# Sliding-window attention with a gated MLP on one core: new durations, a clock model and new priorities for the planner, and four PSUM banks for the first batch's scores

## The chip, the core and the metric

The kernel runs on one core of one Trainium2 chip. The metric is the device time of one execution in microseconds (us), from repeated executions. Five queues of instructions run side by side: TensorE (PE), VectorE (DVE), ScalarE (ACT), GpSimd (POOL) and SyncE (SP), which issues nearly all DMAs. Each runs its own list in order; semaphores hold an instruction back until what it reads is there. PE's results go to PSUM, which has eight banks.

## The reference

Attention over a window with a few sink keys, then an MLP whose hidden layer passes a three-tap convolution gate (`n_sink` 4, `window` 128, batch 4, 8 heads, sequence 768, head 64, `d_model` 512, `d_ff` 1024, all float32):

```python
scores = np.matmul(q, k.transpose(0, 1, 3, 2)) / np.sqrt(D)
keep = (pos[None, :] < n_sink) | ((rel >= 0) & (rel < window))
scores = np.where(keep, scores, -1e9); scores -= scores.max(-1, keepdims=True)
a = np.exp(scores); a /= a.sum(-1, keepdims=True) + 1e-9
x = np.matmul(a, v).transpose(0, 2, 1, 3).reshape(B, S, H * D)
h = np.maximum(x @ w_in, 0)
gate = 1 / (1 + np.exp(-(w0 * h[s - 1] + w1 * h[s] + w2 * h[s + 1])))
out = (h * gate) @ w_out
```

## The kernel before

Heads go in pairs, a *group* g: four groups a batch, sixteen in all. A group has six query tiles of 128 positions, in two halves of three. For a tile t, PE multiplies queries with the keys of two neighbouring tiles and the sinks (`sc`, one for each head of the pair). DVE copies where the window wraps (COPY_PREDICATED) and masks with a minimum (the custom instruction into `pe`), ACT takes the exponential, DVE the sum and its reciprocal, POOL normalises (`pe<-pe,sm`). PE transposes the result (`pts`), ACT copies it to `pT`, POOL cuts it to the window in two selects, and after three tiles PE multiplies with the values (`px`). The sinks' part goes its own way: ACT and DVE split it (`sk`), PE transposes it (`tk`), and it is added to `px`. ACT and DVE split `px` into a high and a low part (`xH`, `xL`). Batch 0 (groups 0 to 3) works in plain float32 and takes the first halves of all four groups first; later batches use pairs of reduced float32 matmuls (`tq`, `kk`, `nq`: keys and queries split and transposed).

The MLP works in *units*, 8 hidden blocks of 128 for each of 12 chunks of 256 positions, 96 in all. A unit's *first* is 12 matmuls into a bank `ph`; its gate passes ACT, ACT, DVE, DVE, ACT, DVE and twice POOL into `g`; its *second* is twice three matmuls from `g` into the two banks `po`, which collect over a chunk's eight units. The input weights come as 64-bit floats: for each of 16 blocks (`wi`, `wo`) and the taps, ACT and DVE turn them into float32 (lines L716 to L718 on DVE) and split them in two (L729: POOL for `wi`, DVE for `wo`). All this runs while batch 0's attention runs, before the first unit can start.

PSUM's eight banks are named places: `h` 2 (ph and the transposes), `po` 2, `sc` 2, `px` 1, `pts` 1. In SBUF there are 4 buffers `g`, 3 `raww` for raw weights, 3 `st`.

The order of everything is made when the kernel is built. `layout` gives each step a priority (`p.at`): a position in steps of score tiles, with fixed offsets: scores at i, transposes at i + 1, `pv` at i + 2, units from i + 3 with seconds TRAIL = 2 unit spans later, weights at 2, 3, 4, and so on. `Plan.run` then goes through all steps as a list scheduler: each step has a busy time and a time until its result is there; the engine that could start earliest takes, among the steps that are ready within `SLACK`, the one of least priority number. `HOP` and `INTO` are times between engines, `SWITCH` a cost on PE, a DMA lands 2300 ns after the fabric moved it. The order that comes out is the program's, on all engines; the chip keeps it.

## Time and profile before

| | |
|---|---|
| median of 3 runs (lowest, highest) | 524.12 us (523.53, 527.19) |
| the profiled execution's own time | 526.89 us |
| its span, first to last instruction | 525.1 us |
| TensorE's mean granted clock | 0.963 |
| busy: PE, DVE, ACT, POOL | 477.2, 341.4, 343.0, 312.4 us |

A page of the profile gives busy times and a strip of 40 slices; the views behind it list waits (which engine stood still, at which line, and who released it), instructions in order of time, and sums by stretch. A matmul's end is modelled, so PE reads as busy through pauses shorter than a matmul's own latency: one matmul of 512 columns is listed with 0.4 us, and twelve of them in a row take 2.9 us.

### The profile page before, as it was taken

Reading aid. Unit: us, or ns where it says so; the run is one execution under the profiler, and the core shown is the slowest. Engines: PE = TensorE matmul, PEld = TensorE weight load, DVE = VectorE, ACT = ScalarE, POOL = GpSimd, SP = SyncE. Lnnn points to the kernel's source line nnn. Section 1 sums busy time; section 2 is a strip of 40 time slices with the busy share of each in tenths; the row PEclk is TensorE's granted clock in tenths of the full one; section 3 lists DMA queues with packets and bytes.
Section 4 is the critical chain, followed back from the end, with each engine's and each line's share of the span. In section 5 each row is a group of like instructions: output and inputs, shape, how many; then the busy total and the mean of one; then the engine's idle time right before and its main releaser. Section 6 shows DMA issues by size and latency. Waiting matters only on the chain.

```text
span 525.1 us, 10461 instructions
## 1 busy us (share of the span) xinstructions
PE 477.2 (91%) x3149; PEld 398.7 (76%) x3149; DVE 341.4 (65%) x1212; ACT 343.0 (65%) x1086; POOL 312.4 (59%) x614
## 2 busy tenths in 40 slices
PE   2867877999999999989999999989999999999994
PEld 2534665878778878877889788878888888898882
DVE  4668898556676676757577766667665764555552
ACT  3867776676777877776687676767766754545541
POOL 3572786565757686675666657565766655344441
PEclk9977679799999999999999999999999999999999
DMA  5848543435332423413233141324030100101001
GB/s 126 237 134 223 172 144 82 114 86 117 88 78 46 117 60 79 106 40 100 47 85 79 31 118 46 81 66 100 1 88 16 41 2 0 42 0 41 23 20 47
DMA packets 87306, 41.01 MB, mean 78 GB/s; under 512 B 80160, under 2 KB 80184, under 8 KB 87240
## 3 DMA queue, kind: packets, MB, share of 16 engines
q1 hardware_dynamic: 87096, 39.99, 29.1%
q8 instruction: 27, 0.44, 0.4%
q14 instruction: 39, 0.32, 0.2%
q10 hardware_dynamic: 144, 0.26, 0.2%
HBM read 27.60 MB, written 6.29 MB: 65 GB/s over the span
## 4 chain that ended last, share of the span: by engine, by line
PE 67%; DVE 12%; POOL 9%; ACT 6%; issue 3%; DMA 2%; SPq 1%; POOLq 0%; ACTq 0%; DVEq 0%
PE ph L776 22%; PE po L807 19%; PE px L1044 8%; PE sc L950 4%; POOL pe L973 4%; PE pts L990 3%; PE sc L953 2%; PE sc L954 2%; PE px L1052 2%; PE tq L914 2%; DVE e L792 1%; DVE a L793 1%; DVE sc L962 1%; DVE kk L891 1%; DVE pe L963 1%
## 5 line engine op out<-in xcount | busy, mean ns | idle before, releaser
L807 PE MATMUL po<-woH,g 128*128 128x512 f32 x384 | 142.3, 407 | 5.5 <-ACT out L612 2.7
L973 POOL TENSOR_SCALAR pe<-pe,sm 128x132 f32<-128x132 f32 (+1 forms) x192 | 88.6, 471 | 64.2 <-DVE sm L971 52.3
L776 PE MATMUL ph<-xH,wiH 128*128 128x258 f32 (+1 forms) x384 | 111.7, 294 | 2.2 <-ACT sT L612 0.9
L776 PE MATMUL ph<-xL,wiH 128*128 128x258 f32 (+1 forms) x384 | 112.9, 296 | 0.0
L776 PE MATMUL ph<-xH,wiL 128*128 128x258 f32 (+1 forms) x384 | 111.6, 293 | 0.0
L796 POOL TENSOR_SCALAR g<-a 128x256 fp32r<-128x256 f32 x96 | 40.4, 421 | 82.3 <-DVE a L795 60.2
L807 PEld LDWEIGHTS po<-woH,g 128*128 128x128 f32 x384 | 71.3, 188 | 23.7 <-POOL g L797 6.2
L967 ACT ACTIVATE pe<-pe,sm 128x132 f32<-128x132 f32 (+1 forms) x192 | 77.1, 403 | 14.1 <-DVE sm L963 13.2
L776 PEld LDWEIGHTS ph<-xH,wiH 128*128 128x128 f32 x384 | 73.7, 192 | 6.6 <-ACT sT L612 1.8
L776 PEld LDWEIGHTS ph<-xL,wiH 128*128 128x128 f32 x384 | 73.8, 192 | 6.4 <-issue 3.4
L776 PEld LDWEIGHTS ph<-xH,wiL 128*128 128x128 f32 x384 | 73.8, 192 | 3.4 <-issue 0.7
L797 POOL TENSOR_TENSOR g<-a,g 128x256 fp32r<-128x256 f32 x96 | 73.3, 763 | 4.8
L807 PE MATMUL po<-woL,g 128*128 128x512 f32 x192 | 75.7, 395 | 0.0
L962 DVE COPY_PREDICATED sc<-before,sc 128x128 f32<-128x128 int32 x160 | 45.8, 291 | 42.3 <-PE sc L954 29.6
L792 DVE SCALAR_TENSOR_TENSOR e<-hb,cw,a 128x256 f32<-128x256 f32 x96 | 50.6, 527 | 34.4 <-ACT a L614 34.0
L610 ACT ACTIVATE hb<-ph 128x258 f32<-128x258 f32 (+1 forms) x96 | 37.0, 385 | 50.3 <-PE ph L776 49.1
L610 ACT ACTIVATE e<-a 128x256 f32<-128x256 f32 x96 | 40.0, 417 | 35.3 <-DVE a L793 34.8
L795 DVE SCALAR_TENSOR_TENSOR a<-e,hb 128x256 f32<-128x256 f32 x96 | 47.4, 493 | 23.4 <-ACT e L610 22.6
L963 DVE CUSTOM_DVE_ANT_0 pe<-sc,m 128x132 f32<-128x132 f32 (+1 forms) x192 | 53.4, 288 | 5.9 <-PE sc L954 2.4
L996 POOL TENSOR_SCALAR_AFFINE_SELECT pT<-pT 128x256 f32<-128x256 f32 x80 | 36.5, 456 | 34.1 <-ACT pT L612 33.0
L793 DVE SCALAR_TENSOR_TENSOR a<-hb,cw,e 128x256 f32<-128x256 f32 x96 | 51.2, 534 | 4.7 <-DVE e L792 0.5
L614 ACT ACTIVATE a<-hb,cw 128x256 f32<-128x256 f32 x96 | 49.0, 511 | 3.2
(168 smaller groups left out, 934.0 us busy)
## 6 DMA issues: line engine op xcount, KB each, us to landing
raw<-in_q_dram SPq DMA_DIRECT2D x64, 96.0 KB
raw<-in_k_dram SPq DMA_DIRECT2D x64, 96.0 KB
out_dram<-out SPq DMA_DIRECT2D x23, 256.0 KB
kk<-kk SPq DMA_DIRECT2D x24, 198.0 KB
vraw<-in_v_dram SPq DMA_DIRECT2D x24, 192.0 KB
roomL<-in_moe_w_in_dram SPq DMA_DIRECT2D x8, 512.0 KB
roomL<-in_moe_w_out_dram SPq DMA_DIRECT2D x8, 512.0 KB
vraw<-in_v_dram SPq DMA_DIRECT2D x8, 128.0 KB
```

The costliest lines, as they stand in the source:

```text
L610: nc.scalar.activation(o, i, func, **({} if scale is None else {"scale": scale}))
L614: nc.scalar.mul(o, i, scale() if callable(scale) else scale)
L776: nc.tensor.matmul(h.ap[:, 0:W], self.wi[i][:, cc, ff * P:(ff + 1) * P], x[k][:, cc, t0:t1], start=(q == 0), stop=(q == len(prods) - 1))
L792: self.dve(324, lambda: stt(out=e.ap, in0=this(), scalar=cw(1), in1=a.ap, op0=ALU.mult, op1=ALU.add), (hb, a), (e,))
L793: self.dve(324, lambda: stt(out=a.ap, in0=nxt(), scalar=cw(2), in1=e.ap, op0=ALU.mult, op1=ALU.add), (hb, e), (a,))
L795: self.dve(266, lambda: stt(out=a.ap, in0=e.ap, scalar=1.0, in1=this(), op0=ALU.add, op1=ALU.mult), (e, hb), (a,))
L797: self.pool(710, lambda: nc.gpsimd.tensor_tensor(out=g.ap[:, 1], in0=a.ap, in1=f(g.ap[:, 0]), op=ALU.subtract), (a, (g, 0)), ((g, 1),))
L807: nc.tensor.matmul(po.ap[:, 0:c.DM], g.ap[:, k, tt * P:(tt + 1) * P], w[:, ff, :], start=(ff == 0 and i == 0), stop=(ff == NFF - 1 and i = ...
L962: self.dve(P, lambda pc=pc: nc.vector.copy_predicated(pc.ap[:, KW:SW], self.before.bitcast(I32), pc.ap[:, 0:P]), ("before", pc), (pc,))
L963: self.dve(n + 14, lambda pc=pc, j=j: nc.vector.tensor_tensor_reduce(out=pe()[:, j, cols], in0=pc.ap[:, P:SW][:, cols], in1=mk, op0=ALU.ad ...
L967: p.op("ACT", 395, 505, lambda j=j: nc.scalar.activation(pe()[:, j, cols], pe()[:, j, cols], AF.Exp, bias=sm[:, j:j + 1], scale=-1.0, accu ...
L973: self.pool(350, lambda j=j: nc.gpsimd.tensor_scalar(pe()[:, j, cols], pe()[:, j, cols], sm[:, 8 + j:9 + j], 1.0, ALU.mult, ALU.mult), ((s ...
```

## The change

It has four parts; no instruction of the kernel is added or taken away beyond semaphores, and no arithmetic changes.

**Durations.** The planner's costs are set anew: times between engines, a scale on each engine's busy times (`SCALE`), an extra `CARE` of 37 ns on each crossing, longer q/k loads, transposes with a shorter busy time, `pv` at twice the cost, DMAs that land 1150 ns after the fabric in place of 2300 + 100, and some single steps.

**The clock.** `Plan.run` keeps a count of PE's busy time in stretches and doubles a matmul's cost where its count says that the clock is halved.

**Priorities.** The offsets in `layout` become a table `LAY` of 22 numbers: among them loads of weights earlier ahead of their conversion (`early` 1.5 to 3.95) and conversions spread wider (4.69 + 1.29 n in place of 2 + n), seconds 5.97 spans behind in place of 2, sinks' loads later (i - 1 to i + 3.44), transposes at i + 1.4.

**Banks.** The scores' place gets the two banks of `po` too, until 36 of its tiles have been taken (18 of batch 0's 24 query tiles); then they go to `po`.

```diff
-HOP = {("PE", "PE"): 0, ("ACT", "ACT"): 92, ("DVE", "DVE"): 104, ("POOL", "POOL"): 83, ("SP", "SP"): 0}
+HOP = {("PE", "PE"): 0, ("ACT", "ACT"): 92, ("DVE", "DVE"): 60, ("POOL", "POOL"): 83, ("SP", "SP"): 0, ("DVE", "POOL"): 160}
-SLACK = {"PE": 40, "ACT": 60, "DVE": 60, "POOL": 60, "SP": 0}
+SLACK = {"PE": 0, "ACT": 35, "DVE": 50, "POOL": 99, "SP": 0}
...
+SCALE = {"PE": 1.0, "ACT": 1.03, "DVE": 1.08, "POOL": 1.12, "SP": 1.0}
+CARE = 37.0
+LENT = 36
...
+    def take(self):
+        self.until -= 1
+        self.line.pop(0)
+        got = self.free.pop(0)
+        if self.until == 0:
+            for x in [x for x in self.free if x[1] in self.lent]:
+                self.free.remove(x)
+                self.owner.free.append(x)
+            self.owner.free.sort(key=lambda y: y[0])
+        return got
...
+            busy, late = o.busy * SCALE[e], o.late * SCALE[e]
+            if e == "PE":
...
+                if slow:
+                    busy, late = 2.0 * busy, late + busy
+                used += busy
...
-                o.end = fabric + 2300.0
+                o.end = fabric + 1150.0
...
+        self.place["po"] = Place("po", 0)
+        self.place["sc"] = Place("sc", 2, ("po_0", "po_1"), self.place["po"], LENT)
...
-        p.at = at + TRAIL * span
+        p.at = at + LAY["trail"] * span
...
+LAY = {"w0": 4.69, "w": 1.29, "early": 3.95, "load": 6.0, "v": 1.6, "prep": 4.71, "span": 1.82, "load2": 8.43, "v2": 2.58,
...
-            m.sinks(g // NP, i - 1)
+            m.sinks(g // NP, i - LAY["sink"])
```

What it does to the order is seen in three places. The first is DVE in batch 0, from the scores of group 3's first tile on (`sc3_0_0`: group 3, tile 0, head 0; `wo0w` is a weight block in conversion, `xL` the low part of a finished `px`). Before:

```order
L963 ISA pe3_0_463,sm4_122<-sc3_0_0_528,m0_124 128x128
L963 ISA sm4_122 128x1
L963 ISA pe3_0_463,sm4_122<-sc3_0_1_532,m0_124 128x128
L963 ISA sm4_122 128x1
L729 TENSOR_TENSOR woL_109<-wo0w_505,woH_108 128x512
L716 TENSOR_SCALAR wo1w_558<-wo1l_547 128x512
L962 COPY_PREDICATED sc3_1_0_543<-before_127,sc3_1_0_543 128x128
L717 SCALAR_TENSOR_TENSOR wo1w_558<-roomL_116,wo1w_558 128x512
L969 TENSOR_REDUCE sm4_122<-sm4_122 128x2
L963 ISA pe3_0_463,sm0_118<-sc3_1_0_543,m1_125 128x132
L963 ISA sm0_118 128x1
L718 SCALAR_TENSOR_TENSOR wo1w_558<-wo1l_547,wo1w_558 128x512
```

And in the changed kernel, from the same scores on:

```order
L999 ISA pe3_0_457,sm4_122<-sc3_0_0_426,m0_124 128x128
L999 ISA sm4_122 128x1
L999 ISA pe3_0_457,sm4_122<-sc3_0_1_429,m0_124 128x128
L999 ISA sm4_122 128x1
L999 ISA pe3_0_457,sm0_118<-sc3_1_0_436,m1_125 128x132
L999 ISA sm0_118 128x1
L999 ISA pe3_0_457,sm0_118<-sc3_1_1_443,m1_125 128x132
L999 ISA sm0_118 128x1
L1006 TENSOR_REDUCE sm3_121<-sm3_121 128x2
L998 COPY_PREDICATED sc3_2_0_468<-before_127,sc3_2_0_468 128x128
L1008 RECIPROCAL sm3_121<-sm3_121 128x2
L999 ISA pe3_0_457,sm1_119<-sc3_2_0_468,m2_126 128x132
```

From `sc3_0_0`'s mask to that of `sc3_2_1` (the last score of the first halves) DVE has 12 conversion steps of `wo0` to `wo3` before and 2, of a `wi` block, now. Up to group 3's first `xL` it has 40 conversion steps before and 25 now, but 9 masks of the second halves' scores where it had 6; up to group 3's second `xL` both kernels have all the conversions, but for the last one of the changed kernel.

The second place is PE in batch 1, around the transpose of the sinks' part (`tk4_2`, group 4), which needs what POOL normalised (as `pts4_2` does) and then ACT and DVE. Before:

```order
L990 MATMUL pts4_2_1603<-ident_85,pe4_0_1296 128x128 x2
L953 MATMUL sc4_4_1_1606<-kk4_948,X41_1286 128x260
L954 MATMUL sc4_4_1_1606<-kk4_948,X41_1286 128x260
L1017 MATMUL tk4_2_1618<-identr_90,sk4_0_1610 72x128
L914 MATMUL tq510_1622<-identr_90,nq51_1371 128x128 x3
```

And now:

```order
L1027 MATMUL pts4_2_1584<-ident_85,pe4_0_1256 128x128 x2
L843 MATMUL po0_1_967<-woH_108,g7_1490 128x512
L843 MATMUL po0_1_967<-woL_109,g7_1490 128x512
L843 MATMUL po0_1_967<-woH_108,g7_1490 128x512
L950 MATMUL tq500_1602<-identr_90,nq50_1311 128x128 x3
L1027 MATMUL pts4_3_1611<-ident_85,pe4_1_1543 128x128 x2
L1054 MATMUL tk4_2_1619<-identr_90,sk4_0_1588 72x128
L989 MATMUL sc4_5_0_1622<-kk4_781,X41_1273 128x260
```

More work stands between the two. Over the 24 such places of batches 1 to 3, at most two scores' pairs of matmuls stood between them in 18 before, and in 6 now.

The third place is PE at the end of the program (`ph95` is the last unit's first, `po88_0<-...,g94` a second of unit 94). Before:

```order
L776 MATMUL ph95_6909<-xL1_1696,wiH_106 128x258
L776 MATMUL ph95_6909<-xH1_1695,wiH_106 128x258
L776 MATMUL ph95_6909<-xH1_1695,wiL_107 128x258
L776 MATMUL ph95_6909<-xL1_1696,wiH_106 128x258
L807 MATMUL po88_0_6807<-woH_108,g94_6953 128x512
L807 MATMUL po88_0_6807<-woL_109,g94_6953 128x512
L807 MATMUL po88_0_6807<-woH_108,g94_6953 128x512
L807 MATMUL po88_1_6814<-woH_108,g94_6953 128x512
L807 MATMUL po88_1_6814<-woL_109,g94_6953 128x512
L807 MATMUL po88_1_6814<-woH_108,g94_6953 128x512
L807 MATMUL po88_0_6807<-woH_108,g95_6970 128x512
```

And now:

```order
L812 MATMUL ph95_6904<-xL1_1840,wiH_106 128x258
L812 MATMUL ph95_6904<-xH1_1839,wiH_106 128x258
L812 MATMUL ph95_6904<-xH1_1839,wiL_107 128x258
L812 MATMUL ph95_6904<-xL1_1840,wiH_106 128x258
L843 MATMUL po88_0_6847<-woH_108,g91_6853 128x512
L843 MATMUL po88_0_6847<-woL_109,g91_6853 128x512
L843 MATMUL po88_0_6847<-woH_108,g91_6853 128x512
L843 MATMUL po88_1_6864<-woH_108,g91_6853 128x512
L843 MATMUL po88_1_6864<-woL_109,g91_6853 128x512
L843 MATMUL po88_1_6864<-woH_108,g91_6853 128x512
L843 MATMUL po88_0_6847<-woH_108,g92_6886 128x512
L843 MATMUL po88_0_6847<-woL_109,g92_6886 128x512
```

Between the last first and the last second stand now the seconds of units 91 to 94, where there was that of 94 alone. Beside the attention of batches 1 to 3 a unit's second comes about four units' firsts behind its own first, where it came about one behind.

## Rows read from the trace of the kernel before

**Rows 1.** The page: the span, and two lines of the strip of 40 slices (PE's busy tenths, and the clock that was granted).

```profile
span 525.1 us, 10461 instructions
PE   2867877999999999989999999989999999999994
PEclk9977679799999999999999999999999999999999
```

**Rows 2.** Busy time by stretch (stretch and its length; busy us and instructions of each engine; granted clock, DMA share, GB/s): batch 0, the middle, the stretch of units alone, the end.

```profile
0.00:105.00 105.00, 78.10 (x381) 56.31 (x382) 75.42 (x262) 69.48 (x208) 61.73 (x116) 0.82 0.57 154
105.00:394.00 289.00, 275.99 (x1975) 236.48 (x1974) 196.71 (x755) 207.96 (x695) 187.36 (x384) 1.00 0.30 75
394.00:517.00 123.00, 121.16 (x791) 104.99 (x789) 68.63 (x196) 64.97 (x184) 62.19 (x114) 1.00 0.06 19
```

**Rows 3.** The same view, the five stretches in which the clock was granted at half.

```profile
29.26:36.08 6.82, 5.09 (x20) 2.75 (x19) 3.46 (x17) 3.26 (x11) 6.27 (x10) 0.50 0.26 86
...
39.49:46.32 6.83, 5.88 (x27) 3.64 (x24) 5.49 (x17) 5.67 (x17) 2.42 (x6) 0.50 0.84 237
...
53.15:63.39 10.24, 9.13 (x29) 6.18 (x31) 8.60 (x36) 7.21 (x22) 7.34 (x13) 0.50 0.50 166
...
70.22:77.04 6.82, 6.22 (x24) 5.07 (x26) 6.82 (x20) 4.66 (x13) 6.45 (x9) 0.50 0.53 171
...
90.70:97.52 6.82, 6.31 (x26) 5.33 (x27) 3.63 (x15) 4.69 (x17) 3.94 (x7) 0.50 0.27 62
```

**Rows 4.** Waits from 0 to 105 us: who waited at which line for whom; us in total, times, the longest.

```profile
POOL pe L973 <- DVE sm L971: 19.5, 7, 6.6
DVE sc L962 <- PE sc L950: 10.9, 13, 2.5
...
PE sc L950 <- DVE sm L963: 7.4, 5, 1.8
...
PE trq L853 <- POOL headscale L636: 6.9, 1, 6.9
```

**Rows 5.** DVE in order of time (start us, us, instruction): the mask of the score `sc3_0_0`, the first and the last of the 12 conversion steps that follow, the mask of `sc3_2_1`, and the `xL` of group 3's two halves.

```profile
42.34 0.29 DVE L963 CUSTOM_DVE_ANT_0 pe<-sc,m 128x128 f32<-128x128 f32 x1 [0.64 <-PE sc L950]
...
42.98 0.69 DVE L729 TENSOR_TENSOR woL<-wo0w,woH 128x512 fp32r<-128x512 f32 x1
...
52.70 0.68 DVE L718 SCALAR_TENSOR_TENSOR wo3w<-wo3l,wo3w 128x512 int32<-128x512 int32 x1
...
53.76 0.29 DVE L963 CUSTOM_DVE_ANT_0 pe<-sc,m 128x132 f32<-128x132 f32 x1
...
65.95 0.56 DVE L1063 TENSOR_TENSOR xL<-px,xH 128x384 fp32r<-128x384 f32 x1
...
126.65 0.56 DVE L1063 TENSOR_TENSOR xL<-px,xH 128x384 fp32r<-128x384 f32 x1 [0.35 <-ACT xH L612]
```

**Rows 6.** PE in order of time: three score matmuls that wait for DVE (in brackets the idle time ahead and who ended it), and the first unit's first matmul.

```profile
50.32 0.68 PE L950 MATMUL sc<-kp,X 128*128 128x260 f32 x2 [1.73 <-DVE sm L963]
51.73 0.68 PE L950 MATMUL sc<-kp,X 128*128 128x260 f32 x2 [0.74 <-DVE sm L963]
...
54.20 1.21 PE L950 MATMUL sc<-kp,X 128*128 128x260 f32 x2 [1.80 <-DVE sm L963]
...
64.22 0.39 PE L776 MATMUL ph<-xH,wiH 128*128 128x258 f32 x1
```

**Rows 7.** PE's waits from 97.5 us to the end.

```profile
PE tk L1017 <- DVE sk L1016: 3.9, 8, 0.8
PE po L807 <- ACT out L612: 2.7, 2, 1.5
PE po L807 <- POOL g L796: 1.5, 1, 1.5
PE tk L1017 <- DVE sm L969: 0.9, 2, 0.5
PE po L807 <- POOL g L797: 0.8, 3, 0.3
```

**Rows 8.** The end of the program in order of time: the last unit's last first, ACT behind it, its POOL step, and PE's first matmul of its second.

```profile
513.48 0.28 PE L776 MATMUL ph<-xL,wiH 128*128 128x258 f32 x1
...
513.80 0.39 ACT L610 ACTIVATE hb<-ph 128x258 f32<-128x258 f32 x1 [1.03 <-PE ph L776]
...
516.96 0.40 POOL L796 TENSOR_SCALAR g<-a 128x256 fp32r<-128x256 f32 x1 [2.35 <-DVE a L795]
...
517.42 0.50 PE L807 MATMUL po<-woH,g 128*128 128x512 f32 x1 [1.54 <-POOL g L796]
```

**Rows 9.** Two pieces of the chain that ended last (start us, us, what): twelve matmuls of seconds, and a wait for a small DMA that had been issued.

```profile
231.59 1.77 DMA vsr<-sinkh
...
498.90 2.90 PE po L807 x12
```

**Rows 10.** The groups of instructions: POOL's first step into `g` (busy us, mean ns; idle time ahead and who ended it).

```profile
L796 POOL TENSOR_SCALAR g<-a 128x256 fp32r<-128x256 f32 x96 | 40.4, 421 | 82.3 <-DVE a L795 60.2 <-PE po L807 7.4 <-DVE sm L971 7.0
```

More of the change, by code (lines that the diff above doesn't have):

```diff
@@ L426 @@
 class Op:
-    __slots__ = ("eng", "busy", "late", "fn", "at", "deps", "soft", "outs", "need", "ready", "turns", "size", "narrow", "start", "end", "n", "what")
+    pass
 class Plan:
@@ L508, in run @@
                 mode = o.narrow
+            busy, late = o.busy * SCALE[e], o.late * SCALE[e]
+            if e == "PE":
+                while t >= window + WINDOW:
+                    slow = used < (0.97 if slow else 0.55) * WINDOW
+                    window, used = window + WINDOW, 0.0
+                if slow:
+                    busy, late = 2.0 * busy, late + busy
+                used += busy
+            o.before = []
             for x in o.turns:
                 if x.slot is None:
-                    x.slot = x.place.free.pop(0)[1]
-                    x.place.line.pop(0)
-            o.start, free[e] = t, t + o.busy
-            o.end = t + o.late
+                    _, x.slot, was = x.place.take()
+                    if was is not None:
+                        o.before.append(was)
+            o.start, free[e] = t, t + busy
+            o.end = t + late
             if o.size:
                 fabric = max(t + o.busy, fabric) + o.size / 225.0
-                o.end = fabric + 2300.0
+                o.end = fabric + 1150.0
             for x in o.turns:
@@ L521, in run @@
                 if not x.left:
-                    x.place.free.append((x.end + 60.0, x.slot))
-                    x.place.free.sort()
+                    x.place.back(x.end + 60.0, x.slot, x)
             for d in o.outs:
@@ L584, in turn @@
         pool = self.ps if kind in ("h", "po", "sc", "px", "pts") else self.sb
-        return Turn(self.place[kind], lambda i: pool.tile(shape, dtype, tag=f"{kind}_{i}", name=name))
+        return Turn(self.place[kind], lambda i: pool.tile(shape, dtype, tag=i if isinstance(i, str) else f"{kind}_{i}", name=name))
     def planes(self, name):
@@ L707, in weight @@
         dst = lambda: raw.ap[0:rows, 0:n * (2 if wide else 1)]
-        self.dma(rows * n * (8 if wide else 4), lambda: nc.sync.dma_start(dst() if not wide else dst().bitcast(I32), src if not wide else src.bitcast(I32)), ("room",), (raw,))
+        self.dma(rows * n * (8 if wide else 4), lambda: nc.sync.dma_start(dst() if not wide else dst().bitcast(I32), src if not wide else src.bitcast(I32)), ("room",), (raw,), busy=410)
         p.at = at
@@ L743, in weights @@
             for cc in range(self.NCC):
-                self.weight(f"wi{half}_{cc}", vi[:, cc, s], ats[n], parts=self.wi, spot=(slice(None), cc, s), engine="POOL")
+                self.weight(f"wi{half}_{cc}", vi[:, cc, s], ats[n], parts=self.wi, spot=(slice(None), cc, s), engine="POOL", early=LAY["early"])
                 n += 1
@@ L749, in weights @@
             for ff in range(HF * half, HF * half + HF):
-                self.weight(f"wo{ff}", vo[:, ff, :], ats[n], parts=self.wo, spot=(slice(None), ff), engine="DVE")
+                self.weight(f"wo{ff}", vo[:, ff, :], ats[n], parts=self.wo, spot=(slice(None), ff), engine="DVE", early=LAY["early"])
                 n += 1
@@ L990, in go @@
                 nc.tensor.transpose(pt.ap[:, j, :], pe.ap[:, u, j, NS:KW], c.ident)
-        self.pe(2 * 108, go, ((pe, u, 0), (pe, u, 1)), (pt,), what=f"pts{g}_{t}")
+        self.pe(170, go, ((pe, u, 0), (pe, u, 1)), (pt,), late=216, what=f"pts{g}_{t}")
         own = self.keytile(s, g, t, hf)
@@ L1090, in layout @@
     st = [Ctx() for g in range(NG)]
-    m.weights([2 + i for i in range(17)])
+    m.weights([LAY["w0"] + LAY["w"] * i for i in range(17)])
     kks = [m.turn("kk", [P, 2, T, KW], F32, f"kp{i}") for i in range(2)]
@@ L1122, in layout @@
             for k in range(n):
-                m.unit(m.NFF * lo + k, i + 3 + span * k / n, span / n)
+                m.unit(m.NFF * lo + k, i + LAY["unit"] + span * k / n, span / n)
 def general(c):
```

76 lines of the change are left out of this document (44 added, 32 removed).

## The prediction

> **What bounds the kernel now.** I read the page first: its strip shows PE full from about a quarter of the span on, and uneven before, where the granted clock falls too [rows 1]. The sums by stretch say it in numbers [rows 2]: in the first 105 us PE is busy for 78.1, in the middle for 276.0 of 289, in the last stretch, where only units are left, for 121.2 of 123. So PE bounds the kernel, and what can be won lies in four places: 26.9 us of PE's idle time in the first 105 us, the half clock there, 13.0 us in the middle, and the end behind 517 us. The half clock comes in five stretches, all in the first 97.5 us; PE is busy in them for 5.09 + 5.88 + 9.13 + 6.22 + 6.31 = 32.6 us, which at the full clock would be 16.3 [rows 3].
>
> Then the waits of the first stretch [rows 4]. The 6.9 us for `headscale` are the program's beginning and stay. The others are one picture: DVE waits 10.9 us for PE's scores, PE 7.4 us for DVE to free a score's bank, POOL 19.5 us for DVE's sums. No engine is full (DVE, the fullest of the helpers, works 75.4 of 105 us [rows 2]); they wait for each other, because each runs its list in order. The timeline of DVE shows why [rows 5]: between the masks of `sc3_0_0` and `sc3_2_1`, at 42.34 and 53.76 us, stand 12 conversion steps of the output weights. PE stands meanwhile at scores three times, 1.73 + 0.74 + 1.80 = 4.3 us, and the first unit starts at 64.22 us [rows 6]. Those weights are not needed before a unit's gate is through. From 97.5 us on PE's waits are short and of a few kinds: 3.9 + 0.9 us at the transposes `tk`, 2.7 us at `po` for the copies out, 1.5 + 0.8 at `po` for `g` [rows 7]; of these the 1.5 is the wait at the very end [rows 8].
>
> **The change part by part.** Nothing is removed from any engine's work, so every gain is a wait that goes, and the sum is one of waits.
>
> *Batch 0's order.* Ten of the 12 conversion steps leave the gap between those two masks. One takes 0.69 or 0.68 us where the timeline shows it [rows 5], the shift among every four less; I take 0.6. Up to group 3's first `xL`, which the first unit needs whole, DVE has 15 conversions less, 9 us, and three scores' masks more, each a copy and a mask of about 0.3 us, 2 us in all: 7 us less DVE work ahead of the first units. The work comes back later: before group 3's second `xL` (at 126.65 us now [rows 5]) both kernels must have done nearly all conversions. There it lies beside the units' matmuls, in the 30 us that DVE idles in this stretch; without that room the 7 us would be paid again.
>
> *Four banks.* With two banks PE can be one tile ahead of DVE; with four, two tiles. That meets the 7.4 us of PE and the 10.9 us of DVE [rows 4], two sides of one thing, so they don't add. At least the 4.3 us of the three waits should mostly go; at most all 10.9. Part of it is the same time as the conversions above, since PE waited for a bank while DVE converted. I take 5 beside the 7. The loan costs the units' seconds nothing as long as the first of them comes after the 18th tile; in the new order it stands behind four units' firsts, so those cover it.
>
> The Trainium skill speaks against this part: "TensorE: Matmul & The Clock Gate", section "HAM oscillation", tells of a kernel in which more PSUM buffers brought no further gain once its matmuls ran without long pauses. By that the 5 us would be 0 and the time 511; the waits for banks listed above say that here the pauses are still there.
>
> *The start together:* 7 + 5 = 12 us. The lower bound is 4 (only the three waits), or 0 if all is given back; the upper is 7 + 10.9, plus a third of the clock's 16.3 us if PE's denser work keeps two of the five half stretches away [rows 3]: 23. That the planner knows the halving moves no work by itself, so it gets no term.
>
> *The middle.* More work now stands between `pts` and `tk`. The waits at `tk` come where ACT's and DVE's small steps take longer than what stands there; such places fall from 18 to 6 of 24, so I take two thirds of 4.8 us: 3.2. The seconds stand four units behind their firsts in place of one, which takes away the 0.8 us at `po` for `g`. Together 4. Against it: new priorities can make new waits anywhere, and the planner now believes that a DMA lands 1.15 us after the fabric, where the chain has 1.77 us of waiting behind a small one's issue [rows 9]. Sinks are loaded later too, so three batches may each stand 0.6 us or more. Bounds: 3 lost (these and as much again) to 12 won (nearly all of PE's 13.0 us idle [rows 2]).
>
> *The end.* The last first ends 0.12 us after 513.48 (its neighbours' spacing, since 12 seconds take 2.90 us at 512 columns [rows 9] and these have half), the last second starts at 517.42 [rows 8]: 3.8 us for the gate's chain through ACT, DVE and POOL, covered by six seconds, 1.45 us. Now 24 seconds stand there, 5.8 us, and the chain is hidden: 2.4 us won. What is late next is only the copy and store of the last tiles, which stay. Bounds 1.5 (the wait that is listed) and 2.4.
>
> *Sum:* 12 + 4 + 2.4 = 18.4 us. From the profiled execution's own time, 526.89 us, that gives 508.5. This execution was 2.8 us above the median of the three runs, 524.12; from the median it is 505.7, and I say 506.
>
> **The rivals.**
>
> *Given back.* DVE's deferred conversions, 15 of 59, return before group 3's second `xL`. If PE then waits for scores as it did before, only later, the 12 us go and the middle and the end remain: 524.1 - 6.4 = 517.7. For it: all conversions but one are still ahead of that `xL`. Against it: PE has units to run by then, and DVE's idle 30 us are four times the 7.
>
> *More than that.* DVE's whole wait for scores goes and the clock stays up longer: 23 us in the start, with the rest 29: 494.5. For it: all three engines wait for each other [rows 4], so one loosened link moves all. Against it: the chain from a score through POOL to `px` is as long as it was.
>
> *Slower: the buffers of `g`.* There are four. With seconds four units behind, POOL's step into `g` of unit n needs the buffer that the second of unit n - 4 frees, at about the time when the first of unit n is done. POOL runs in order, so its normalising of scores waits behind that step, then `pts`, `pT`, `px`. Before, POOL already waited 7.4 us for this [rows 10]. Some 64 units run beside attention. If 0.29 us of such waiting reached PE at each, the 18.4 us would be lost; at 0.5 us each, 32 us, the time is 524.1 - 18.4 + 32 = 538. Against it: POOL has 100 us of idle time in the 289 us of the middle [rows 2], and the planner holds these buffers in its account.
>
> **How the numbers follow.** The sum as worked out, with its start between 6 and 17 and a middle between 0 and 8: 0.67, 498 to 514, at 506. Given back: 0.14, 514 to 522, about 518. More: 0.11, 488 to 498. Slower: 0.08, 525 to 545. A measurement tells about 1%, 5.2 us, from no change. Faster than 518.9 are the first and the third and about a third of the second: 0.83; the rest of the second and what of the fourth stays under 529.4 is within: 0.10; slower 0.07. The range 495 to 518 leaves out the slower case, part of the second and the best of the third.
>
> **What would show it.** In the new profile the first unit should start at 50 to 57 us in place of 64.22, group 3's second `xL` come 8 to 17 us before 126.65, PE's waits for DVE at scores fall below 3 us, and DVE's for PE's scores by half. The middle should list under 2 us at `tk`, and the end no wait of PE for `g`. If the first unit is early but that `xL` is not, it was given back. If POOL lists far more than 7.4 us of waits for PE at its step into `g` and PE waits at `pts` for POOL in the middle, it is the buffers. The forecast is wrong at its root if the first unit isn't earlier.

## The result, and the profile after

The changed kernel takes 478.48 us (median of 4 runs, 478.36 to 478.63), the kernel before 525.46 on the same chip: a ratio of 0.911 (95% interval 0.907 to 0.915). The forecast was 506 us within 495 to 518. The direction was right; the gain is 47 us, not 18.

The page of the changed kernel, span and strip; against [rows 1] PE is busy for 0.8 or more of every slice from the second to the last but one, and the clock stands at full up to the last slice:

```profile
span 476.7 us, 10474 instructions
PE   3898889999999999999999999999999999999995
PEclk9999999999999999999999999999999999999998
```

To see where the 48.4 us between the two profiled spans come from, both are cut at work that is the same in both: the first unit's first matmul, DVE's write of the last `xL` of batch 0 (mark A, group 3's second half), and its write of the last `xL` of all (mark Z, the end of attention). Before, they stand at 64.22 [rows 6], 126.65 [rows 5] and 444.99 us:

```profile
444.99 0.56 DVE L1063 TENSOR_TENSOR xL<-px,xH 128x384 fp32r<-128x384 f32 x1 [3.25 <-ACT xH L612]
```

The same three in the timeline of the changed kernel:

```profile
43.86 0.36 PE L812 MATMUL ph<-xH,wiH 128*128 128x258 f32 x1
...
101.49 0.55 DVE L1101 TENSOR_TENSOR xL<-px,xH 128x384 fp32r<-128x384 f32 x1
...
397.44 0.56 DVE L1101 TENSOR_TENSOR xL<-px,xH 128x384 fp32r<-128x384 f32 x1 [0.84 <-ACT xH L648]
```

So 25.2 us are won up to A, 318.3 - 296.0 = 22.4 from A to Z, and 80.1 - 79.3 = 0.8 behind Z. Busy time by stretch between the marks (columns as in [rows 2]), before:

```profile
0.00:126.65 126.65, 98.20 (x524) 73.00 (x525) 89.51 (x318) 84.96 (x260) 75.36 (x145) 0.85 0.55 145
126.65:444.99 318.34, 306.59 (x2189) 263.94 (x2188) 212.32 (x819) 223.53 (x747) 205.81 (x419) 1.00 0.25 64
444.99:525.10 80.11, 72.40 (x438) 61.80 (x436) 39.62 (x77) 34.49 (x81) 31.21 (x50) 0.99 0.08 28
```

and after:

```profile
0.00:101.49 101.49, 83.13 (x532) 63.54 (x532) 86.65 (x315) 78.75 (x254) 78.74 (x145) 1.00 0.68 173
101.49:397.44 295.95, 293.52 (x2169) 256.05 (x2170) 222.83 (x824) 225.86 (x754) 211.72 (x420) 1.00 0.29 71
397.44:476.70 79.26, 73.74 (x450) 65.66 (x449) 41.36 (x75) 34.24 (x80) 32.49 (x50) 0.98 0.08 29
```

The middle row holds the lesson of this case. PE's *busy* time falls by 13.1 us in it and its idle time by 9.3, from 11.75 to 2.43. But the row has 20 matmul records fewer (2189 and 2169), so part of the 13.1 us is work that now stands elsewhere. The second products show it. Before, between A and Z and behind Z:

```profile
126.65:444.99 318.34, 103.83 (x386) 67.21 (x385) 0.00 (x0) 9.20 (x16) 1.00 0.25 64
444.99:525.10 80.11, 41.71 (x154) 26.16 (x152) 0.69 (x1) 3.93 (x7) 0.99 0.08 28
```

and after (a matmul that lies across a mark is counted on both sides):

```profile
101.49:397.44 295.95, 103.17 (x364) 62.02 (x365) 0.00 (x0) 9.05 (x16) 1.00 0.29 71
397.44:476.70 79.26, 48.12 (x174) 29.25 (x173) 0.69 (x1) 4.06 (x7) 0.98 0.08 29
```

Counted by their starts, the stretch from A to Z has 385 `po` matmuls before and 364 after, 280 and 276 of scores, 772 of `ph` in both; the stretch behind Z has 20 of `po` more and 8 of `ph` fewer. At 0.24 us for one of `po` (2.90 / 12 [rows 9]) and 0.12 for one of `ph` or of scores (half the columns), that is an estimated 5.5 us of work less from A to Z, 3.8 more behind Z and 1.7 more up to A. *At equal work* the three gains are then about 27, 17 and 4.7 us. Of the middle's 17, 9.3 came out of listed idle time and about 7.6 out of time that the profile calls busy: nearly half. The weight loads (second pair of numbers in the rows by stretch), whose time is stretched less (one for `po` lasts 188 ns in the mean before and 189 after), leave 54.4 us of the stretch free before and 39.9 after. The Trainium skill says this of the measure itself: "Perfetto Trace Analysis", section "Identifying the Most-Contended Engine", calls the busy share of matmuls no good measure of how close one is to the peak, because matmuls are pipelined, and names the weight loads' busy share among the measures to take instead; the rows here agree (busy share 96% before, weight loads 83%).

PE's waits in the changed kernel, first from 0 to 105 us (against [rows 4]), then from 97.5 us on (against [rows 7]):

```profile
PE trq L889 <- POOL headscale L672: 6.9, 1, 6.9
PE pts L1027 <- POOL pe L1010: 2.2, 4, 1.1
...
PE sc L986 <- DVE sm L1008: 1.0, 1, 1.0
PE sc L986 <- DVE sm L999: 0.8, 1, 0.8
...
PE tk L1054 <- DVE sk L1053: 1.3, 3, 0.5
PE tq L950 <- ACT hb L646: 0.6, 1, 0.6
```

The waits at scores are down from 7.4 to 1.8 us, those at `tk` from 4.8 to 1.3, and the wait for `g` at the end [rows 8] is not there. DVE's wait for PE's scores, 10.9 us in [rows 4], is 0.2. Ahead of the first unit, PE and DVE before:

```profile
0.00:64.22 64.22, 43.30 (x188) 28.22 (x188) 43.39 (x172) 41.38 (x127) 33.21 (x76) 0.81 0.64 178
```

and after:

```profile
0.00:43.86 43.86, 31.61 (x185) 23.35 (x185) 31.75 (x157) 33.57 (x116) 29.27 (x72) 1.00 0.76 196
```

For as many matmuls PE is 11.7 us less busy, which is about the half clock's share (half of 5.09 + 5.88 + 9.13 is 10.05 us [rows 3]), and DVE does 11.6 us less work first.

### The profile page after: what moved, and what is told of

It is laid out like the page before. It is cut to its first block, busy times and chain, and to the rows that moved or that the text cites. A ratio compares the mean times of both kernels' runs of the same rounds, so it can differ in the third digit from the quotient of the medians.

```text
span 476.7 us, 10474 instructions
## 1 busy us (share of the span) xinstructions
PE 450.4 (94%) x3149; PEld 385.2 (81%) x3149; DVE 350.8 (74%) x1212; ACT 338.9 (71%) x1086; POOL 322.9 (68%) x614
## 4 chain that ended last, share of the span: by engine, by line
PE 67%; DVE 15%; ACT 7%; POOL 6%; issue 2%; DMA 1%; POOLq 0%; SPq 0%; DVEq 0%; ACTq 0%
PE ph L812 25%; PE po L843 21%; PE px L1081 7%; PE pts L1027 3%; PE sc L989 3%; PE sc L990 3%; POOL pe L1010 2%; ACT pe L1004 2%; DVE kk L927 2%; PE tq L950 2%; DVE e L828 2%; ACT kk L648 1%; DVE pe L999 1%; PE px L1089 1%; DVE a L831 1%
## 5 line engine op out<-in xcount | busy, mean ns | idle before, releaser
L843 PE MATMUL po<-woH,g 128*128 128x512 f32 x384 | 149.4, 407 | 0.0
L812 PE MATMUL ph<-xL,wiH 128*128 128x258 f32 (+1 forms) x384 | 111.6, 291 | 0.0
L1010 POOL TENSOR_SCALAR pe<-pe,sm 128x132 f32<-128x132 f32 (+1 forms) x192 | 90.2, 481 | 30.6 <-DVE sm L1008 20.5
L832 POOL TENSOR_SCALAR g<-a 128x256 fp32r<-128x256 f32 x96 | 41.8, 435 | 84.2 <-DVE a L831 36.4
L833 POOL TENSOR_TENSOR g<-a,g 128x256 fp32r<-128x256 f32 x96 | 80.2, 835 | 4.2
L843 PEld LDWEIGHTS po<-woH,g 128*128 128x128 f32 x384 | 72.5, 189 | 10.8 <-POOL g L833 0.3
L828 DVE SCALAR_TENSOR_TENSOR e<-hb,cw,a 128x256 f32<-128x256 f32 x96 | 57.1, 595 | 29.1 <-ACT a L650 28.1
L831 DVE SCALAR_TENSOR_TENSOR a<-e,hb 128x256 f32<-128x256 f32 x96 | 47.6, 495 | 20.9 <-ACT e L646 20.5
L829 DVE SCALAR_TENSOR_TENSOR a<-hb,cw,e 128x256 f32<-128x256 f32 x96 | 56.7, 591 | 5.2
L998 DVE COPY_PREDICATED sc<-before,sc 128x128 f32<-128x128 int32 x160 | 43.9, 287 | 12.1 <-PE sc L990 10.9
L1033 POOL TENSOR_SCALAR_AFFINE_SELECT pT<-pT 128x256 f32<-128x256 f32 x80 | 38.5, 481 | 12.8 <-ACT pT L648 12.6
L646 ACT ACTIVATE hb<-ph 128x258 f32<-128x258 f32 (+1 forms) x96 | 36.9, 384 | 14.3 <-PE ph L812 13.0
```

The costliest lines, as they stand in the source:

```text
L646: nc.scalar.activation(o, i, func, **({} if scale is None else {"scale": scale}))
L812: nc.tensor.matmul(h.ap[:, 0:W], self.wi[i][:, cc, ff * P:(ff + 1) * P], x[k][:, cc, t0:t1], start=(q == 0), stop=(q == len(prods) - 1))
L828: self.dve(324, lambda: stt(out=e.ap, in0=this(), scalar=cw(1), in1=a.ap, op0=ALU.mult, op1=ALU.add), (hb, a), (e,))
L829: self.dve(324, lambda: stt(out=a.ap, in0=nxt(), scalar=cw(2), in1=e.ap, op0=ALU.mult, op1=ALU.add), (hb, e), (a,))
L831: self.dve(266, lambda: stt(out=a.ap, in0=e.ap, scalar=1.0, in1=this(), op0=ALU.add, op1=ALU.mult), (e, hb), (a,))
L833: self.pool(710, lambda: nc.gpsimd.tensor_tensor(out=g.ap[:, 1], in0=a.ap, in1=f(g.ap[:, 0]), op=ALU.subtract), (a, (g, 0)), ((g, 1),))
```

## The experiments

Each kernel is one of the two with the edit shown. "Undone" means set back inside the change. The table gives the median, the ratio to the kernel before on the same chip with its 95% interval, and the marks of the profiled execution (us). The last column is the gain from A to Z against the kernel before at equal work, estimated as above from the counts of `po`, `ph` and score matmuls between the marks of each run. Some expectations count by stretches of fixed time, so that their shares differ from the table's.

| run | median | ratio | first unit | A | Z | A to Z | won there at equal work |
|---|---|---|---|---|---|---|---|
| before | 525.46 | 1 | 64.22 | 126.65 | 444.99 | 318.3 | 0 |
| change | 478.48 | 0.911 (0.907-0.915) | 43.86 | 101.49 | 397.44 | 296.0 | 16.9 |
| e1 loan undone | 483.39 | 0.921 (0.917-0.925) | 48.85 | 104.13 | 402.49 | 298.4 | 16.1 |
| e2 priorities undone | 506.74 | 0.966 (0.961-0.970) | 58.73 | 113.92 | 425.88 | 312.0 | 6.6 |
| e3 all costs undone | 496.01 | 0.945 (0.941-0.949) | 46.52 | 103.66 | 413.67 | 310.0 | -1.8 |
| e4 loan alone | 524.34 | 0.998 (0.995-1.001) | 63.80 | 125.18 | 442.40 | 317.2 | -0.6 |
| e5 halving undone | 479.92 | 0.912 (0.909-0.916) | 46.42 | 105.78 | 399.88 | 294.1 | 17.8 |
| e6 durations undone | 504.48 | 0.958 (0.954-0.963) | 47.35 | 105.80 | 421.03 | 315.2 | -6.7 |
| e7 weights undone | 487.45 | 0.928 (0.924-0.932) | 48.17 | 111.31 | 405.22 | 293.9 | 17.9 |
| e8 distance undone | 494.26 | 0.941 (0.937-0.945) | 43.69 | 102.74 | 413.18 | 310.4 | 5.0 |
| e9 distance alone | 512.85 | 0.977 (0.972-0.982) | 61.97 | 119.72 | 430.73 | 311.0 | 4.9 |
| e10 clock held | 523.13 | 0.995 (0.993-0.998) | 60.33 | 121.03 | 441.45 | 320.4 | -2.1 |
| e11 attention undone | 479.50 | 0.912 (0.908-0.916) | 46.13 | 104.22 | 398.11 | 293.9 | 18.0 |
| e12 preparation, fills undone | 485.06 | 0.922 (0.919-0.926) | 52.05 | 106.52 | 403.97 | 297.5 | 15.0 |
| e13 transfers undone | 489.41 | 0.931 (0.926-0.936) | 44.76 | 101.27 | 409.21 | 307.9 | 5.4 |
| e14 pv undone | 480.78 | 0.915 (0.910-0.920) | 45.92 | 105.57 | 399.34 | 293.8 | 16.6 |
| e15 hops, slacks undone | 491.73 | 0.937 (0.932-0.943) | 45.49 | 104.38 | 408.56 | 304.2 | 8.4 |
| e16 single steps undone | 485.14 | 0.923 (0.917-0.929) | 48.02 | 106.39 | 401.36 | 295.0 | 14.7 |
| e17 five buffers of g | 478.38 | 0.914 (0.909-0.918) | 44.25 | 101.77 | 395.80 | 294.0 | 17.1 |
| e18 loan to 44 | 481.07 | 0.919 (0.914-0.924) | 43.80 | 100.29 | 399.16 | 298.9 | 17.5 |

The runs stand on several chips, and the intervals of e5, e11, e14, e17 and e18 overlap the change's: what sets these five apart from it is not clear of noise.

**The parts, e1 to e4.** e1, no loan:

```diff
-        self.place["po"] = Place("po", 0)
-        self.place["sc"] = Place("sc", 2, ("po_0", "po_1"), self.place["po"], LENT)
```

> The changed kernel with the scores' place left at its own two banks and po at its own two from the start; all else of the change stays. If the four banks carry the start (theory B), the clock falls to half again in batch 0, the first unit starts after 52 us in place of 43.9, and the time goes up by 10 us or more, to 489 or above. If priorities and costs carry it (theory P and theory C), the order closes most of the gap by itself: 479 to 485 us, with the clock at full.

e2, the 22 numbers of `LAY` as they were:

```diff
-LAY = {"w0": 4.69, "w": 1.29, "early": 3.95,
+LAY = {"w0": 2.0, "w": 1.0, "early": 1.5,
...
-       "prep2": 3.86, "span2": 3.05, "tr": 1.4, "pv": 1.68, "unit": 2.44, "trail": 5.97,
+       "prep2": 6.0, "span2": 5.0, "tr": 1.0, "pv": 2.0, "unit": 3.0, "trail": 2.0,
```

> The changed kernel with the 22 priorities set back to those of before (weights at 2 + n with loads 1.5 ahead, seconds 2 spans behind, sinks at i - 1 and so on); the new costs, the clock model and the loan of banks stay. If the priorities carry the gain (theory P), most of the 47 us goes: 505 us or more, with half-clock stretches in batch 0 and waits at tk and po for g in the middle. If the true costs carry it (theory C), the list scheduler makes a good order from old priorities too: 480 to 492 us.

e3, all the numbers of the costs as they were, and no halving:

```diff
-SLACK = {"PE": 0, "ACT": 35, "DVE": 50, "POOL": 99, "SP": 0}
+SLACK = {"PE": 40, "ACT": 60, "DVE": 60, "POOL": 60, "SP": 0}
...
-                if slow:
+                if False:
...
-                o.end = fabric + 1150.0
+                o.end = fabric + 2300.0
```

> The changed kernel with the planner's costs of before (times between engines, no scale and no extra care, old slack, old single durations, DMAs landing at 2300 + 100) and without its clock model; the new priorities and the loan stay. Theory P: 480 to 492 us, since the priorities decide what goes first. Theory C: 505 us or more, and the loss shows in the middle as well as in the start.

e4, the kernel before with the loan:

```diff
+        self.place["po"] = Place("po", 0)
+        self.place["sc"] = Place("sc", 2, ("po_0", "po_1"), self.place["po"], LENT)
```

> The kernel before with nothing but the loan of the two banks. Theory B: the start shortens by 5 to 11 us, 513 to 519 us, and DVE's wait for PE's scores in the first 105 us halves. Theories P and C: within 3 us of before, since the conversions still stand between the scores on DVE.

Against the change, the loan is worth 4.9 us, the priorities 28.3, the costs 17.5. These add up to 50.7 where the whole change brings 47.0. The loan alone brings nothing that can be told from no change (e4). Priorities and loan with the old costs (e3) bring 23 of the 25.2 us up to A; between A and Z they bring 8.3 us by the marks and, at equal work, nothing: e3 has 32 `po` and 12 `ph` matmuls fewer there than the kernel before. Its time lies between the ranges of its two theories. The new costs and the loan with the old priorities (e2) bring half of the start and 6.6 us of the middle, where the whole change wins 17: from A to Z the two need each other. Without the loan PE waits at scores for DVE's sums again in the stretch ahead of e1's first unit:

```profile
PE sc L984 <- DVE sm L997: 4.3, 7, 1.7
```

In the old order (e4) 11 conversions still stand between the masks where [rows 5] has 12. PE's wait for DVE at the scores falls from 7.4 to 5.2 us up to 105 us, but its wait for POOL at `px` rises from 1.5 to 3.4, and nothing of it reaches the end.

**The costs taken apart, e5, e6, e13 to e16.** e5, no halving; e6, the rest of e3's numbers old and the halving kept:

```diff
-                if slow:
+                if False:
```

> The change with one thing undone: the plan no longer doubles a TensorE duration where it reckons with the half clock. The corrected durations, the new priorities and the loan of two banks stay. The old durations and no halving together cost 17.5 us, all of it in the middle (105 to 394 us). Theory D (the durations alone make the middle): 478 to 483 us, and the gain at each stretch as in the change. Theory K (the halving makes it, because it moves what the plan lays beside the first units): 488 to 497 us, with the start as in the change (first unit at 43 to 48 us) and the middle's gain gone from 28 us back to about 26.

> The change with the other half of the costs undone: the old durations, hops and slacks are back, the halving of the clock, the new priorities and the loan stay. Theory D: 490 to 498 us, a start as good as the change's (first unit at 44 to 49 us), and a middle that adds nothing to it. Theory K: 478 to 484 us.

The halving is worth at most the 1.4 us of e5 with the new durations (theory D; theory K is out), and with the old ones it does harm: 504.5 with it (e6, above the ranges of both theories), 496.0 without (e3). So the durations carry the middle. They were then set back in four groups: e13 `fabric + 2300.0` and `o.end + 100.0`, the issue times and the size of a load; e14 `P / 1.2` for `P / 0.6`; e15 `HOP`, `SLACK`, `SCALE` and `CARE`; e16 some single steps (transposes, a copy, two selects).

> The change with one group of its corrected numbers undone, those of transfers: a transfer lands 2400 ns after its bytes in place of 1150, and the issue times and the size of a load are the old ones. All groups together cost 26 us where the halving stays, 17.5 where it goes too. Theory S (the engines' hops, slacks and scales carry the middle): 478 to 483 us here. Theory M (the transfers' do): 488 to 500 us, with TensorE waiting for the sinks' transfers again (4.6 us with all groups undone).

> The change with one number set back: the products with v are planned at half their length again (128 columns divided by 1.2 in place of 0.6, so 107 in place of 213 ns for each block). Theory S: 478 to 483 us. Theory V (TensorE's own plan runs ahead of the engine by this, and everything laid beside it comes late): 486 to 498 us, the loss all after 105 us.

> The change with one group of numbers undone: the hops between engines, the slacks in which an engine may take a later step, the scales of 3 to 12 per cent on ScalarE, VectorE and GpSimd, and 37 ns for a crossing. Theory S: 488 to 502 us, with TensorE's waits for VectorE at the scores back in the middle. Theories M and V: 478 to 484 us.

> The change with one group of numbers undone: six single durations (transposes on TensorE planned longer again, two masks on GpSimd 10 to 95 ns shorter, the copy of a turned q 95 ns shorter). Theories S, M and V: 478 to 483 us. If small errors add up whatever their kind: 483 to 490 us, here and in the other three.

They cost 10.9, 2.3, 13.3 and 6.7 us, 33.2 in all where all together cost 26.0. Between A and Z, at equal work, it is the transfers (11.5 us) and the hops and slacks (8.5); the single steps cost 2.2 and the product with v 0.3 there, more in the start (4.9 and 4.1 up to A). So theories S and M hold side by side, theory V falls, and no single group is the cause. Two forecasts missed: e15 has the time of theory S but not its sign (PE's waits for DVE at the scores in the middle are 0.5 us), and e16 lies outside the 478 to 483 us of all three theories, in the range of small errors that add up, which e14's 480.8 doesn't bear out. With the transfers' numbers old, PE waits for a transfer in the middle again, which it doesn't in the change:

```profile
PE px L1089 <- DMA vsr<-sinkl: 7.5, 3, 3.7
```

Two of these waits, 3.74 us up to 118.70 and 2.51 up to 206.02, are followed by a stretch at half clock, of which the change has none before its end:

```profile
118.70 0.30 PE L1089 MATMUL px<-sT,vsr 72*128 72x128 f32 x1 [3.74 <-DMA vsr<-sinkl]
...
118.97:122.38 3.41, 3.41 (x15) 3.14 (x14) 2.79 (x13) 3.31 (x13) 1.79 (x5) 0.50 0.81 246
...
206.02 0.30 PE L1089 MATMUL px<-sT,vsr 72*128 72x128 f32 x1 [2.51 <-DMA vsr<-sinkl]
...
207.72:211.14 3.42, 3.42 (x16) 3.21 (x15) 2.31 (x10) 2.51 (x10) 2.55 (x5) 0.50 0.28 93
```

PE is busy through both, so they cost an estimated half of their 6.8 us at most, 3.4. With the 7.5 us of waits that makes up to 10.9 of the 11.5 us. e3 and e6 have such stretches in their middles too (6.8 and 10.2 us long in all), both of e6's and one of e3's at a wait for the same transfer.

**The distance of the second products, e8, e9, e17.** e8 sets one number back, e9 sets it alone in the kernel before, e17 gives `g` a fifth buffer:

```diff
-"trail": 5.97
+"trail": 2.0
```

> The change with one priority set back: the second product of a unit stands 2 units behind the first again, not 5.97. Theory T (the distance between a unit's two products frees the middle of waits for g): the start as in the change, TensorE's waits for g of 1 us or more back and the middle slower, 484 to 498 us, and 2 to 3 us lost at the end. Rival theory: the place of the second product is set by data and by the buffers of g, 478 to 482 us, with a start as in the change.

> The kernel before with one priority new: the second product of a unit stands 5.97 units behind the first, not 2. Old durations, no halving, the other 21 priorities old, two banks for the scores. In the change this priority alone is worth 15.8 us (494.3 against 478.5), nearly all of it after 105 us. Theory R (a stock of ready second products fills TensorE's pauses, whatever the rest is): 508 to 515 us, the start as before (first unit at 63 to 65 us), 8 to 12 us won between 105 and 394 us and 2 to 3 at the end. Rival theory (the stock pays only where the plan's durations are true): 519 to 525 us.

```diff
-NGB = TRAIL + 2
+NGB = TRAIL + 3
```

> The change with five buffers of g in place of four, so that the stock of ready second products can grow by one. GpSimd waits 15.0 us for a buffer of g between 105 and 394 us in the change, TensorE not at all for g. Theory R (the stock fills TensorE's pauses, and it is full enough): 477 to 480 us. If the stock is still too small: 470 to 476 us. If it crowds out the scores: above 481 us.

This one number is worth 15.8 us: by the marks 14.5 of them between A and Z, at equal work about 12 there and 3.6 behind Z. Theory T's place and size were right, its sign on the trace was not: in e8 PE waits 2.9 us for `g` in the whole run, 2.0 of them at the very end; between 105 and 480 us it is the scores' banks, `tk` and other transposes that it waits for. The busy time between A and Z goes up by 8.5 us, for work (17 of `po` more, 8 of `ph` and 4 of scores fewer) that explains an estimated 2.6 of them:

```profile
102.74:413.18 310.44, 302.06 (x2174) 260.75 (x2173) 212.37 (x813) 224.83 (x746) 205.19 (x417) 1.00 0.27 67
```

What the number does is seen on POOL, in its waits from 105 to 394 us ahead of `g`. In the change it waits for PE to use up an older `g`:

```profile
POOL g L832 <- PE po L843: 15.0, 17, 3.5
```

In e8 it waits for its input, and never that long for PE:

```profile
POOL g L832 <- DVE a L831: 32.3, 22, 5.2
```

Counted from the rows (the end of the nth step L833 that fills a `g`, against the start of the nth unit's first `po` matmul), a finished `g` lies for a median of 12.8 us in the change between 200 and 300 us, and for 1.0 in e8, 0.5 before. PE has a stock of second products that wait for nothing, which can be laid where PE would else wait for a score, a transpose or a sink. With the old number they are used up as soon as they can be. The timeline of PE in e8 shows a place where none was left:

```profile
252.22 0.28 PE L989 MATMUL sc<-kk,X 128*128 128x260 f32 x1
252.34 0.28 PE L990 MATMUL sc<-kk,X 128*128 128x260 f32 x1
253.21 0.45 PE L950 MATMUL tq<-identr,nq 128*128 128x128 f32 x3 [0.59 <-ACT hb L646]
253.81 0.23 PE L1054 MATMUL tk<-identr,sk 128*72 128x128 f32 x1 [0.15 <-DVE kk L927]
253.93 0.41 PE L1027 MATMUL pts<-ident,pe 128*128 128x128 f32 x2
254.67 0.36 PE L989 MATMUL sc<-kk,X 128*128 128x260 f32 x1 [0.33 <-DVE sm L999]
```

It shows too where busy time hides a pause. Scores of this shape start 0.12 us apart when nothing holds them, but each row lasts 0.28. From 252.34 to 253.21 PE lost 0.75 us, and 0.59 are listed; by that a pause under 0.16 us isn't listed at all.

e9 puts a limit on theory R: alone the stock brings 12.2 us (13.9 between the two profiled spans), at equal work about 4.9 between A and Z where 8 to 12 were expected, 4.5 up to A where none was, and 4.5 behind Z. So a stock is not enough. Counted in the same way a `g` lies for 14.1 us in e9, 13.6 in e3 and 14.3 in e6, as long as in the change, and with the old durations e3 wins nothing in the middle and e6 loses 6.7 us. That the new durations let the plan lay the stock into PE's true pauses fits all of these runs; it was not followed place by place, and a smaller stock with the new priority was not tried. e17 says that the stock is full enough: POOL's waits for PE at `g` fall from 15.0 to 0.3 us, a `g` lies for 15.4, the time stays (478.4).

**The start, e7, e10 to e12, e18.** Priorities set back, e7 `w0`, `w`, `early`; e11 `tr`, `pv`, `soft`, `xs`; e12 `v`, `prep`, `span`, `vs`, `zeros`, `vsr`, `sink`:

```diff
-"w0": 4.69, "w": 1.29, "early": 3.95
+"w0": 2.0, "w": 1.0, "early": 1.5
...
-"tr": 1.4, "pv": 1.68, "soft": -1.03, "xs": 0.57
+"tr": 1.0, "pv": 2.0, "soft": 0.0, "xs": 0.0
...
-"v": 1.6, "prep": 4.71, "span": 1.82, "vs": -0.17, "zeros": 5.11, "vsr": 17.96, "sink": -3.44
+"v": 2.0, "prep": 2.5, "span": 2.0, "vs": 1.2, "zeros": 3.2, "vsr": 10.0, "sink": 1.0
```

> The change with 3 of its 22 priorities set back, those of the weights' loads and splits (first load at 2.0 in place of 4.69, one each 1.0 in place of 1.29, splits 1.5 ahead in place of 3.95). Theory W (the start is won because the weights' work stands behind the first batch's scores): the first unit slips by 6 to 14 us, a half-clock stretch or two come back ahead of 105 us, 486 to 500 us. Rival theory O (other priorities win it: preparation, transposes, the units' place): first unit at 43 to 48 us, 478 to 484 us.

> The change with 4 priorities set back: the transposes of a step at 1.0 behind its scores in place of 1.4, the products with v at 2.0 in place of 1.68, and the two offsets for the exponentials and for the write of x (-1.03 and 0.57) at 0. Theory A (what a step does behind its scores is where the start's other half lies): first unit at 48 to 56 us, 484 to 494 us. Rival theory (the order of these follows from data, the priorities hardly move it): first unit at 43 to 47 us, 478 to 482 us.

> The change with 8 priorities set back, all of the first batch: the loads of v and the preparation of q and k (2.0, 2.5, 2.0 in place of 1.6, 4.71, 1.82; the loads of q and k are the same in both), and the zero fills on GpSimd with the sinks' loads (vs, zeros, vsr, sink). Theory F (they hold up the first steps): first unit at 48 to 56 us, 484 to 494 us. Rival theory: first unit at 43 to 47 us, 478 to 482 us.

The weights' place is worth 9.0 us (first unit 4.3 later, A 9.8 later), preparation and fills 6.6 (first unit 8.2 later, A 5.0 later), the steps behind the scores no more than 1.0. Theory F holds, theory A falls; of theory W the time and the half-clock stretches hold (two are back ahead of 105 us), the slip of 6 to 14 us doesn't. At A the losses of e7, e12, e11 and e1 (9.8, 5.0, 2.7, 2.6) make 20.2 of the 25.2 us; the rest wasn't taken apart.

e10, the kernel before with transposes of the unit matrix where PE waited:

```diff
+    fill = {("sc", 2): 12, ("sc", 10): 4, ("sc", 14): 14, ("pv", 1): 10, ("pts", 7): 4, ("pts", 8): 8, ("sc", 23): 14, ("sc", 24): 6,
+            ("sc", 25): 15, ("sc", 32): 14, ("pts", 14): 5}
...
+            for i in range(fill.get((kind, k), 0)):
+                c.nc.tensor.transpose(keep[:, 0:P], c.ident, c.ident)
             o.fn()
```

> The kernel before in its own order, with 106 transposes of the unit matrix laid ahead of eleven of the places where TensorE waited in the first batch; they write a po bank that is not in use yet, about 11 us of work in pauses of about 12 us. Nothing else is moved, and no result is touched. Theory L (the half clock itself holds the start up): the half-clock stretches between 29 and 77 us, 31 us in all, go or shrink to under 10 us, the first unit starts 8 to 14 us earlier, 510 to 517 us. Theory N (at half clock TensorE only fills time in which it would wait for VectorE and ScalarE): the stretches go, the first unit stays at 60 to 65 us, 521 to 527 us. If the stretches stay, the run tells nothing of either, 524 to 535 us.

Its strip shows the clock at full where it had been at half four times [rows 1, 3]. It stays there up to 87.0 us; two stretches at half of 3.4 us each follow, from 87.0 and from 343.0 us. The waits ahead of the first unit, at 60.33 us, are other ones:

```profile
PEclk9999998999999999999999999989999999999999
```

```profile
PE px L1044 <- POOL pT L998: 2.4, 3, 1.4
PE pts L990 <- POOL pe L973: 2.0, 3, 1.0
PE sc L950 <- DVE sm L963: 1.1, 2, 1.0
```

Theory N: ahead of the first unit the half clock costs PE about 10 us of work, and with the clock held 3.9 of them reach the first unit, 5.6 reach A, and the medians on that chip (523.13 and 525.04) are 1.9 apart. In the old order the half clock mostly filled time in which PE would have waited for POOL and DVE; 11 us of filling work found room in it. Two things make 1.9 us a lower bound of what a held clock is worth there: the transposes may have held up PE's own work here and there, and 2.1 us are lost again from A to Z, where the stretch at 343 us is new.

e18 prolongs the loan:

```diff
-LENT = 36
+LENT = 44
```

> The change with the two banks lent for the first 44 score banks, not 36. Theory B (the banks still bound the first batch's scores): first unit at 40 to 44 us, 474 to 478 us. Rival theory (the first second products wait for the banks): first unit as in the change, the first second product later, 479 to 486 us.

The first unit stays, the first `po` matmul comes at 75.93 us in place of 59.70, and the kernel is 2.6 us slower, at the edge of what can be told: the rival's case. No run beats the changed kernel; e17 equals it.

## Why the prediction was wrong in size

Two terms failed, by about as much: the start (12 us, upper bound 23; 25.2 measured, about 27 at equal work) and the middle (4 us, upper bound 12; 22.4 by the marks, about 17 at equal work). The direction and the parts named were right.

**Batch 0's order (7 us): right mechanism, too small, and one term at nothing.** Where I counted 15 conversions less up to group 3's first `xL`, DVE does 11.6 us less work ahead of the first unit. But that is one of two mechanisms: the weights' priorities are worth 9.0 us by e7 (9.8 at A), and the preparation of q and k with POOL's fills, to which I gave no term, 6.6 by e12 (5.0 at A). I had read the one gap that the waits pointed at [rows 4 to 6] and not the others that the same table moves.

**Four banks (5 us): right, 4.9 in e1,** but only in the new order; alone none (e4, ratio 0.998, interval 0.995 to 1.001). What the section "HAM oscillation" of the Trainium skill's "TensorE: Matmul & The Clock Gate" tells of another kernel, that more PSUM buffers gave no further gain, is so here in e4 and not in e1.

**The clock: no term for the planner's halving was right** (at most 1.4 us, e5). That the half stretches all vanish is what the order did, and it is worth little by itself: e10 holds the clock up to 87 us without the order and wins 1.9 us, 5.6 up to A. That is the size of the 5 us in the upper bound, and not the 10 us that PE's busy time suggests.

**The middle (4 us, bounds -3 to 12): the step whose reasoning failed.** It brought 22.4 us between A and Z, about 17 at equal work. The term for `tk` was right: 3.2 forecast, 3.5 won. The distance of the seconds I priced by the waits for `g` that it removes, 0.8 us; undoing it costs about 12 of the 17 (e8), since ready products can serve any wait of PE, not those for `g` alone. And the bound was false: "nearly all of PE's 13.0 us idle" took listed idle time for all that there was to win, while about 7.6 us lay in the rows' busy time. The new costs I counted as a risk only; without them all of the 17 go (e3). So neither gives more than a part of the middle without the other: the distance with old durations wins 4.9 us at most (e9), the new costs with the old distance 5.0 (e8), with all priorities old 6.6 (e2).

**The end (2.4 us): by the marks 0.8.** The wait for `g` at the end went as forecast. The stretch behind Z holds 20 `po` matmuls more than before and 8 of `ph` fewer, 3.8 us of work; with it the gain behind Z is an estimated 4.7. That is about 2 us more than forecast; where they lie in these 80 us was not followed.

**The rivals.** Given back: the gain is 25.2 us at A and 47.6 at Z, so it fell. The buffers of `g`: POOL waits 23.4 us for PE there in the whole run (15.0 from 105 to 394 us) against 7.4 in [rows 10], as that rival said; none of it reaches PE, whose waits for POOL in the middle are not listed at all, and a fifth buffer changes nothing. More than that: right in direction, and still 16 us short (its terms add up to 494.7, not 494.5), because it left the middle at 4 us and the start at 23.

**What was to be seen.** First unit at 50 to 57: 43.86. Group 3's `xL` 8 to 17 us earlier: 25.2. PE's waits at scores under 3 us: 1.8. DVE's halved: 10.9 to 0.2. At `tk` under 2: 1.3. No wait for `g` at the end: none. Every sign held; both sizes of the start were passed.

What stays open: the 11.5 us that the old transfers' numbers lose between A and Z are nearly all seen in the waits for sinks and the half clock behind them; the 8.5 us by the hops and slacks (e15), where the clock stays full, were not followed to their places.

## What to carry to other kernels

Where an engine is the bound and runs pipelined work, don't bound a gain by its listed idle time: compare its busy time for the same work between two marks (count the work by tile: here 20 of 2189 matmuls had moved, an estimated 5.5 us), or the spacing of its rows' starts with the closest spacing of that shape. Work that is ready and wanted late (here second products) is worth keeping in stock, here four units deep, for whatever the bound engine would wait for; it is priced by all waits, not by its own, and it paid in full only with the new durations. Correct a planner's durations together with its priorities: the halving of the clock was harmless with the new durations and cost 8.5 us with the old ones.

## What was not expected of the hardware

PE reads 96% busy between A and Z before and still had about 17 us to give in 318, an estimated 7.6 of them out of rows that read as busy. A clock at half for 31 us ahead of the first `po` matmul [rows 3], held at full by 11 us of transposes in PE's pauses, moved the end by 0.5% (interval 0.2 to 0.7%). And the waits for the sinks in e13, 7.5 us as listed, cost up to 10.9 with the half clock that followed two of them.
